# A fused attention and expert kernel: q's softmax subtraction, exponential and sum issued behind k's steps of the same unit

## The chip, the cores and the metric

The kernel runs on one core of one Trainium2 chip. The metric is the device time of one execution in microseconds, and the smaller is the better. Names of engines: PE is the matrix engine (TensorE), DVE is VectorE, ACT is ScalarE, POOL is GpSimd, SP is SyncE.

## What is computed

Three stages follow each other. Linear attention on q, k and v of 8 batches, 8 heads, 576 positions and 64 columns; a mixture of 8 experts with one expert per token; and a second, gated network. Cut to what matters:

```python
def _attn_ref(q, k, v):
    q_s = np.exp(q - np.max(q, axis=-1, keepdims=True))
    q_s = q_s / (np.sum(q_s, axis=-1, keepdims=True) + 1e-09)
    k_s = np.exp(k - np.max(k, axis=2, keepdims=True))
    k_s = k_s / (np.sum(k_s, axis=2, keepdims=True) + 1e-09)
    kv = np.einsum('bhsd,bhse->bhde', k_s, v)
    return np.einsum('bhsd,bhde->bhse', q_s, kv)
...
logits = x @ w_gate; e_idx = np.argmax(logits, axis=1)
out[mask] = gate_w * sigmoid(x @ w_output_gate)[e] * (np.maximum(x[mask] @ w1[e], 0) @ w2[e])
...
h = np.maximum(np.maximum(x @ w1, x @ w2), x @ w3); result = h @ w_out
```

The softmax of q goes over the 64 columns of a head, that of k over the 576 positions. x has 4608 tokens of 512 columns; an expert has 1024 hidden columns, the second network 768, and its weights come as float64 bits that the core decodes.

## The kernel before, in words

The attention works in units of half a batch's heads. Unit n is batch n // 2, half n % 2; even units are first halves, odd units second halves. The steps of a unit are small functions. For q: q_max, q_exp (L224 to 229: on DVE the subtraction of the maximum over 128 x 1280 elements, L228, then the exponential on ACT, L229), q_sum (L255 to 262, three DVE operations: the sum L259, and L260 and L261 on its 20 columns), q_norm (L264, DVE) and, for each of the two pairs of heads, q_tr (L315: PE transposes L320, ACT copy L327) and q_lo (L330, DVE L335: the low part of the transposed q). For k: k_max, k_tr (L231: PE transposes L236, DVE maximum L238 and two multiplications L241 that make dg), k_exp (L245: PE product of ones and dg L248, DVE subtraction L251, ACT exponential L253), kv_mm, kv_norm and kv_lo. Then x_mm (L337: PE products L353, ACT copies L361 and L363) and x_lo (L365, DVE L371) give the tokens of a pair, and logit_mm and logit_tr (PE L390, ahead of it ACT copies L384 and L385 in the last pair of a batch) feed the router, whose steps are route_1 to route_5; route_1 has six DVE instructions (L399 to L410), and route_5 is a POOL scatter into a table in memory (L489), five of them per batch.

Beside this the expert that most tokens of a batch chose is computed for all its tokens. Its work is cut in groups of 12 products of 128 x 288 (three per pair of operands, since each operand is split in a high and a low part). l1_group (PE L611) ends in an ACT operation (L616) and a DVE one (L617) that write h; l2_group (L629) reads h and ends on ACT (L634) in a batch's first half of groups and on DVE (L636) in its second half. 32 groups make a batch: 8 of l1, 8 of l2, and both again. The weights are split by ACT (L588) and POOL (L595). Between them dec_bits and dec_store decode weights of the second network (DVE L677 to 681 and L694, POOL L685, L686, L695).

One group is a slot. Behind each group moe_slot calls run_events, which issues all steps that a table has put at that slot. Engines work through their instructions in the order of issue; no scheduler moves them. The table is written by hand: START[n] = 16 n - 51 is a unit's slot 0, STEADY (L44) gives the offsets of its steps for units 4 to 15 and EARLY those of units 2 and 3; batch 0 has a list of its own. So k_tr stands at offset 0 of its unit, k_exp at 1, kv_mm and kv_norm at 6, q_norm at 8. The steps of a unit's second pair of heads come at offsets 15 to 19, which are offsets -1, 0, 1, 2 and 3 of the next unit: q_tr, q_lo, x_mm, x_lo and logit_mm of the previous unit. Behind the next even unit's offset 4 follow logit_tr and route_1. From offset 3 on, up to 10, the groups are l1 groups; those at -5 to 2 are l2 groups.

The table is read here:

```python
    FRONT = (q_max, q_exp, k_max, k_tr, k_exp, q_sum, kv_mm, kv_norm, kv_lo, q_norm)
    BACK = (q_tr, q_lo, x_mm, x_lo, logit_mm)
    for n, s0 in START.items():
        ...
        for d, f in zip(t[0], FRONT):
            if d is not None:
                at(s0 + d, f, b, hb)
```

Of the kernel before, what the change touches and what calls it, by code (L numbers as in the profile page):

```python
# [16 lines left out]
PSUM = bass.MemoryType.PSUM  # L17
# [11 lines left out]
CAP = 96  # L29
SLOT = 64  # L30
# [4 lines left out]

# batches whose attention output comes from plain float32 products instead of three with split operands
NFULL = 2

# The order of the work beside the experts' matrix products, in slots of one group of 12 products; a unit is
# half of a batch's heads. STEADY: slots after a unit's START for the steps in FRONT, and those in BACK for  # L40
# each pair of heads; EARLY: the same for the first units, from the first slot on. LOAD: a unit's loads.
# ROUTE: the router's steps after START of a batch's second unit, for batch 0 and 1 from the first slot on.
# DEC: pieces of the float64 weights, after START of even units, of odd units and of the last one.
STEADY = ((-4, -1, -4, 0, 1, 3, 6, 6, 7, 8), (10, 10, 13, 14, 15), (15, 16, 17, 18, 19))  # L44
EARLY = {
# [11 lines left out]
def tile_linear_attention__then__moe(  # L57
# [21 lines left out]

# [1 line left out]
    const = ctx.enter_context(tc.tile_pool(name="const", bufs=1))  # L81
# [24 lines left out]

# [1 line left out]
    es_moe = ExitStack()  # L108
# [20 lines left out]

# [1 line left out]
    def setup():  # L131
# [40 lines left out]

# [1 line left out]
    units = {}  # L174
# [197 lines left out]

    # the logits with tokens as columns: column tile c of the array takes tokens 128 c on; the last 64 follow on tile 0
    def logit_mm(b, hb, pr):
# [17 lines left out]

# [1 line left out]
    def route_1(b):  # L394
# [60 lines left out]
    def route_4(b):  # L455
        pool = nc.gpsimd
        r = rt[b]
        oh, cs, nm = r["oh"], r["cs"], r["nm"]
        cb = cbuf[b % 2]
        for c in range(4):  # L460
            pool.tensor_tensor(out=cb[:, c + 1], in0=cb[:, c], in1=cs[:, 0, c], op=ALU.add)
        n_b = n_all[:, E * b:E * b + E]
        s_b = st_all[:, E * b:E * b + E]
        pool.tensor_tensor(out=n_b, in0=r["cnt"], in1=nm[:, 0], op=ALU.mult)
        pool.tensor_copy(pad_a[:, 4:12], n_b)
        pool.tensor_tensor(out=pad_b[:, 4:12], in0=pad_a[:, 4:12], in1=pad_a[:, 3:11], op=ALU.add)
        pool.tensor_tensor(out=pad_a[:, 4:12], in0=pad_b[:, 4:12], in1=pad_b[:, 2:10], op=ALU.add)
        pool.tensor_tensor(out=pad_b[:, 4:12], in0=pad_a[:, 4:12], in1=pad_a[:, 0:8], op=ALU.add)
        pool.tensor_tensor(out=s_b, in0=pad_b[:, 4:12], in1=n_b, op=ALU.subtract)
        pool.tensor_tensor(out=s_b, in0=s_b, in1=base.to_broadcast([128, E]), op=ALU.add)  # L470
        pool.tensor_tensor(out=base, in0=base, in1=pad_b[:, 11:12], op=ALU.add)
        mo = sm.tile([128, 5, E], F32, tag="rmo", name="rmo")
        pool.tensor_tensor(out=mo, in0=oh, in1=nm.to_broadcast([128, 5, E]), op=ALU.mult)
        a = sm.tile([128, 5, E], F32, tag="ra", name="ra")
        pool.tensor_tensor(out=a, in0=cs[:, 1], in1=cb[:, 0:5], op=ALU.add)
        pool.tensor_tensor(
            out=a, in0=a, in1=s_b.rearrange("p (o e) -> p o e", o=1).to_broadcast([128, 5, E]), op=ALU.add
        )
        # the position of a token that leaves its batch's majority expert; BIG for the others
        pool.tensor_scalar(out=a, in0=a, scalar1=-float(BIG), scalar2=None, op0=ALU.add)  # L480
        pool.tensor_tensor(out=a, in0=a, in1=mo, op=ALU.mult)
        for w in (4, 2, 1):
            pool.tensor_tensor(out=a[:, :, 0:w], in0=a[:, :, 0:w], in1=a[:, :, w:2 * w], op=ALU.add)
        pi = sm.tile([128, 5], I32, tag="rpi", name="rpi")
        pool.tensor_scalar(out=pi, in0=a[:, :, 0], scalar1=float(BIG), scalar2=None, op0=ALU.add)
        r["pi"] = pi
# [6 lines left out]

# [1 line left out]
    events = {}  # L495
# [55 lines left out]

# [1 line left out]
    raw_t = {}  # L553
# [98 lines left out]

# [1 line left out]
    dec = deque((i, j) for j in range(8) for i in range(4))  # L654
# [12 lines left out]
    def dec_bits():  # L667
        if not dec_r:
            return
        i, j, raw = dec_r.popleft()  # L670
        lo, hi = raw[:, :, 0], raw[:, :, 1]
        f = dc_p.tile([128, 384], I32, tag="df", name="df")
        p = dc_p.tile([128, 384], I32, tag="dp", name="dp")
        a2 = dc_p.tile([128, 384], F32, tag="da", name="da")
        r = dc_p.tile([128, 384], F32, tag="dr", bufs=2, name="dr")
        # sign, exponent less 896 and the upper 20 bits of the mantissa
        vec.tensor_scalar(out=f, in0=hi, scalar1=0x07FFFFFF, scalar2=3,  # L677
                          op0=ALU.bitwise_and, op1=ALU.logical_shift_left)
        vec.scalar_tensor_tensor(out=f, in0=hi, scalar=-0x40000000, in1=f,
                                 op0=ALU.bitwise_and, op1=ALU.bitwise_or)  # L680
        vec.tensor_scalar(out=p, in0=f, scalar1=-0x00800000, scalar2=None, op0=ALU.bitwise_and)
        act(out=a2, in_=hi.bitcast(F32), func=ACTF.Abs)
        # the lower 32 bits, added with one rounding
        act(out=r, in_=lo.bitcast(U32), func=ACTF.Copy, scale=2.0 ** -52)
        nc.gpsimd.tensor_tensor(out=r, in0=r, in1=p.bitcast(F32), op=ALU.mult)  # L685
        nc.gpsimd.tensor_tensor(out=r, in0=r, in1=f.bitcast(F32), op=ALU.add)  # L686
        dec_m.append((i, j, a2, r))

    def dec_store():
        if not dec_m:  # L690
            return
        i, j, a2, r = dec_m.popleft()
        # under float32's range, by the upper word (0x38100000 and on, read as a float): zero
        vec.tensor_scalar(out=a2, in0=a2, scalar1=1.125 * 2.0 ** -15, scalar2=None, op0=ALU.is_ge)  # L694
# [9 lines left out]

# [1 line left out]
    m_all = [t.rearrange("p j n -> (p j n)").rearrange("(k f) -> k f", f=F2) for t in w32_d[0:3]]  # L706
# [29 lines left out]

    # ================= program =================
    with tc.manual_schedule():
# [95 lines left out]

# [1 line left out]
        sl = {}  # L836

        def fx_table():
# [43 lines left out]
            vec.tensor_reduce(out=sf[:, 0:4], in_=pr, axis=AX.X, op=ALU.add)  # L882
            # start = valid * (start0 + SLOT * j)
            vec.tensor_scalar(out=sf[:, 4:5], in0=jc, scalar1=float(SLOT), scalar2=None, op0=ALU.mult)
            vec.scalar_tensor_tensor(
                out=sf[:, 2:3], in0=sf[:, 4:5], scalar=sf[:, 3:4], in1=sf[:, 2:3], op0=ALU.mult, op1=ALU.add
            )
            # static start = min(start + CAP * (1 - valid), CAP)
            vec.tensor_scalar(
# [3 lines left out]
            vec.tensor_scalar(out=sf[:, 3:4], in0=sf[:, 4:5], scalar1=float(CAP), scalar2=None, op0=ALU.min)  # L893
            # trips of the general loop: 0 where the static slots cover everything
            nsl = incl[:, w - 1:w]
# [55 lines left out]

        # half a piece of a minority expert's weights: 256 rows of 512 columns
        def fx_w(e_reg, i):
# [33 lines left out]

        # the tokens' upper and lower parts side by side: the first pass multiplies both with the
        # weights' upper part, the second the upper part with the weights' lower part
        def fx_mm(ps, x, ws, kh):  # L990
# [9 lines left out]

        # adds the two parts and turns tokens to columns
        def fx_sum(raw):
# [62 lines left out]

        # steps between the groups of the second network; one that leaves its sum open in PSUM comes
        # only where the next step follows before that bank is needed again
        fix = deque((f, False) for f in (fx_table, fx_gather, fx_soft, lambda: None, fx_tr))
# [12 lines left out]

        # chunks: (sources of y, N, list of (scale, writer))
        def chunk_l2(c, hs, part=0):
# [20 lines left out]

        # chunk B holds the last 64 tokens of each batch, in two parts; the second carries the packed tokens
        order = [(c, 0) for c in range(B)] + [(B, 0), (B, 1)]
# [113 lines left out]
```

## Time and profile before

| what | value |
|---|---|
| time, median of 3 runs | 1252.41 us (1251.85 to 1254.42) |
| span of the profiled execution | 1248.6 us |
| between the two | 3.8 us |
| PE busy | 1193.2 us, 96% |
| DVE busy | 647.8 us, 52% |
| ACT busy | 447.0 us, 36% |
| POOL busy | 380.4 us, 30% |

The span is that of one execution, recorded by the hardware profiler; the durations below come from it. The profile has one time per run of instructions, the wait ahead of it and what ended that wait. A busy time counts an instruction from its start to its end, also when something held it in between. A granted clock of 1.00 is PE's full speed, 2.4 GHz, and 0.50 is 1.2 GHz.

### The profile page before, as it was taken

What the parts mean: (1) busy time and instruction counts of PE and PEld (TensorE: products, weight loads), DVE (VectorE), ACT (ScalarE), POOL (GpSimd) and SP (SyncE); (2) the same over time, 40 slices, a digit from 0 to 9 for tenths busy, and PEclk for the clock granted to TensorE, in tenths of its full rate; (3) what the DMA queues carried; (4) which work ended last, traced back from release to release, by engine and by line L of the source; (5) the groups of instructions that cost most, each with busy time, mean ns of one, the idle gap of its engine ahead of it and who ended that gap; (6) DMA issues with size and microseconds to landing.
All of it is one profiled execution on the core that took longest, in us unless ns stands there. A gap on an engine that the chain in (4) does not pass through costs nothing. (4 is left out here: it accounts for less than half of the span.)

```text
span 1248.6 us, 19283 instructions
## 1 busy us (share of the span) xinstructions
PE 1193.2 (96%) x7518; PEld 1054.4 (84%) x7518; DVE 647.8 (52%) x1161; ACT 447.0 (36%) x864; POOL 380.4 (30%) x466
## 2 busy tenths in 40 slices
PE   4699999999999999999999999999999999999996
PEld 3598998989899898999888888888888888888995
DVE  7779787787878789534442414132331313232211
ACT  2463554546454554534331223122232213221211
POOL 1257767676776667772002000000000000000000
PEclk9799999999999999999999999999999999999998
DMA  6776555675665544353512121211222111210001
GB/s 167 183 198 175 166 176 159 175 214 148 202 202 164 170 128 148 123 188 99 169 35 79 36 67 52 83 44 34 85 68 76 46 56 51 51 51 1 35 17 24
DMA packets 141455, 135.68 MB, mean 109 GB/s; under 512 B 70045, under 2 KB 104637, under 8 KB 140336
## 3 DMA queue, kind: packets, MB, share of 16 engines
q1 hardware_dynamic: 139648, 134.01, 36.1%
q8 instruction: 61, 1.00, 0.3%
q0 software_dynamic: 1712, 0.39, 0.2%
q14 instruction: 34, 0.28, 0.1%
HBM read 106.99 MB, written 27.62 MB: 108 GB/s over the span
## 5 line engine op out<-in xcount | busy, mean ns | idle before, releaser
L813 PE MATMUL pm<-yh,wf 128*128 128x512 f32 (+2 forms) x2160 | 464.8, 375 | 0.0
L813 PEld LDWEIGHTS pm<-yh,wf 128*128 128x128 f32 x2160 | 385.9, 188 | 72.5
L629 PE MATMUL yp<-h,w 128*128 128x288 f32 x1536 | 226.3, 303 | 0.2 <-DVE h L617 0.2
L611 PE MATMUL hp<-xs,w 128*128 128x288 f32 x1536 | 218.9, 299 | 0.0
L629 PEld LDWEIGHTS yp<-h,w 128*128 128x128 f32 x1536 | 212.1, 192 | 3.6 <-DVE h L617 0.5
L611 PEld LDWEIGHTS hp<-xs,w 128*128 128x128 f32 x1536 | 208.1, 190 | 2.8 <-POOL w L595 0.2
L595 POOL TENSOR_TENSOR w<-stg,w 128x512 fp32r<-128x512 f32 x126 | 179.4, 1427 | 77.0 <-ACT w L588 74.9
L820 DVE TENSOR_TENSOR tm<-tm,pm 128x512 f32<-128x512 f32 (+2 forms) x60 | 38.6, 643 | 256.6 <-ACT tm L819 152.3
L1077 POOL DMA_INDIRECT out_dram<-oc,ftb x1 | 1.0, 983 | 548.4 <-ACTq L1149 548.4
L831 PE MATMUL op<-wo,hc 128*128 128x512 f32 (+1 forms) x666 | 152.8, 390 | 0.0
L831 PEld LDWEIGHTS op<-wo,hc 128*128 128x128 f32 (+1 forms) x666 | 124.5, 187 | 26.3
L819 ACT ACTIVATE tm<-pm 128x512 f32<-128x512 f32 (+2 forms) x60 | 33.7, 562 | 230.9 <-PE pm L813 230.2
L617 DVE SCALAR_TENSOR_TENSOR h<-hp,h 128x288 fp32r<-128x288 f32 x128 | 56.6, 451 | 58.8 <-ACT h L616 58.5
L616 ACT ACTIVATE h<-hp 128x288 fp32r<-128x288 f32 x128 | 52.2, 408 | 84.6 <-PE hp L611 84.2
L588 ACT ACTIVATE w<-stg 128x512 fp32r<-128x512 f32 x128 | 78.8, 621 | 0.0
L823 ACT ACTIVATE hc<-tm 128x512 fp32r<-128x512 f32 (+2 forms) x60 | 35.8, 597 | 93.9 <-DVE tm L821 93.9
L824 DVE TENSOR_TENSOR hc<-tm,hc 128x512 fp32r<-128x512 f32 (+2 forms) x60 | 38.9, 649 | 39.8 <-ACT hc L823 39.8
L833 ACT ACTIVATE oc<-op,tsrc 128x512 f32<-128x512 f32 x32 | 22.1, 689 | 101.9 <-PE op L831 101.9
L489 POOL DMA_INDIRECT tab_d<-tsrc,rpi x40 | 45.9, 1147 | 37.5 <-DMA tab_d<-tsrc,rpi 26.2
L685 POOL TENSOR_TENSOR dr<-dr,dp 128x384 f32<-128x384 f32 x32 | 32.5, 1015 | 53.2 <-ACT h L616 37.3
L228 DVE TENSOR_TENSOR q<-q,qm 128x1280 f32<-128x1280 f32 x15 | 42.7, 2849 | 0.0
L821 DVE TENSOR_TENSOR tm<-tm,pm 128x512 f32<-128x512 f32 (+2 forms) x60 | 38.6, 644 | 7.0 <-DVE tm L820 0.9
(219 smaller groups left out, 1179.1 us busy)
## 6 DMA issues: line engine op xcount, KB each, us to landing
stg<-in_moe_w_dram SPq DMA_DIRECT2D x31, 1024.0 KB, 5.7
fw<-in_moe_w_dram SPq DMA_DIRECT2D x24, 512.0 KB, 3.8
v<-in_v_dram SPq DMA_DIRECT2D x80, 128.0 KB, 4.8
draw<-in_moe_w_dram SPq DMA_DIRECT2D x24, 384.0 KB, 4.1
y_d<-y SPq DMA_DIRECT2D x32, 288.0 KB, 2.7
k<-in_k_dram SPq DMA_DIRECT2D x16, 512.0 KB, 5.2
q<-in_q_dram SPq DMA_DIRECT2D x16, 512.0 KB, 6.6
yr<-y_d SPq DMA_DIRECT2D x8, 1024.0 KB, 5.2
```

The source lines that it names most:

```text
L228: eng.tensor_tensor(out=qt, in0=qt, in1=u["qm"].to_broadcast([128, 20, D]), op=ALU.subtract)
L489: nc.gpsimd.indirect_dma_start(out=tab_d[:, :], out_offset=bass.IndirectOffsetOnAxis(ap=rt[b]["pi"][:, c:c + 1], axis=0), in_=tsrc[:, b, c ...
L588: act(out=t[:, 0], in_=src, func=ACTF.Copy)
L595: eng.tensor_tensor(out=t[:, 1], in0=src, in1=t[:, 0].bitcast(F32), op=ALU.subtract)
L611: mm(ps, w[:, a, kk], xp[b, kk][:, c, cs], start=(n == 0), stop=(n == 11))
L616: act(out=h[:, 0, cs], in_=ps, func=ACTF.Relu)
L617: vec.scalar_tensor_tensor(out=h[:, 1, cs], in0=ps, scalar=0.0, in1=h[:, 0, cs].bitcast(F32), op0=ALU.max, op1=ALU.subtract,)
L629: mm(ps, w[:, a, f], ht[f][:, c, cs], start=(n == 0), stop=(n == 11))
L813: mm(pp[m][:, 0:n], wf[f][:, a, m, kk], ys[kk][:, c, 0:n], start=(kk == 0 and i == 0), stop=(kk == 3 and i == 2))
L820: vec.tensor_tensor(out=tv, in0=tv, in1=pp[1][:, 0:n], op=ALU.max)
L824: vec.tensor_tensor(out=h[:, 1, 0:n], in0=tv, in1=h[:, 0, 0:n].bitcast(F32), op=ALU.subtract)
L831: mm(ps[0:m], hs[f][:, a, 128 * t:128 * t + m], wo[f][:, c], start=(i == 0), stop=(i == 17))
```

## The change

In STEADY the offset of q_exp goes from -1 to 2 and that of q_sum from 3 to 5. All else stays (the other lines of the diff take comments out, and the line numbers hold for both).

```diff
-STEADY = ((-4, -1, -4, 0, 1, 3, 6, 6, 7, 8), (10, 10, 13, 14, 15), (15, 16, 17, 18, 19))
+STEADY = ((-4, 2, -4, 0, 1, 5, 6, 6, 7, 8), (10, 10, 13, 14, 15), (15, 16, 17, 18, 19))
```

The order of issue changes on DVE and ACT in units 4 to 15; on PE, POOL and SP it is the same. First, DVE around offset 0 of an odd unit, before. The rows name line, operation, tiles and shape; q and qm are the unit's q and its maximum, qTs the transposed q of the previous unit's second pair, dg k's maxima on a diagonal, xs the tokens, y and h the expert's tiles.

```order
L371 TENSOR_TENSOR xs<-xr,xs 128x576
L636 TENSOR_TENSOR y<-yp,y 128x288
L228 TENSOR_TENSOR q<-q,qm 128x1280
L636 TENSOR_TENSOR y<-yp,y 128x288
L335 TENSOR_TENSOR qTs<-qT,qTs 128x576
L238 TENSOR_REDUCE m_3381<-kT 128x2
L241 TENSOR_SCALAR dg<-ident,m_3381 128x128 x2
L636 TENSOR_TENSOR y<-yp,y 128x288
L251 TENSOR_TENSOR k<-k,kB 128x1280
L636 TENSOR_TENSOR y<-yp,y 128x288
L371 TENSOR_TENSOR xs<-xr,xs 128x576
L617 SCALAR_TENSOR_TENSOR h<-hp,h 128x288
```

The same place after the change, from the q_lo of the previous unit on:

```order
L335 TENSOR_TENSOR qTs<-qT,qTs 128x576
L238 TENSOR_REDUCE m_3379<-kT 128x2
L241 TENSOR_SCALAR dg<-ident,m_3379 128x128 x2
L636 TENSOR_TENSOR y<-yp,y 128x288
L251 TENSOR_TENSOR k<-k,kB 128x1280
L636 TENSOR_TENSOR y<-yp,y 128x288
L371 TENSOR_TENSOR xs<-xr,xs 128x576
L228 TENSOR_TENSOR q<-q,qm 128x1280
L617 SCALAR_TENSOR_TENSOR h<-hp,h 128x288
L677 TENSOR_SCALAR df<-draw 128x384
L679 SCALAR_TENSOR_TENSOR df<-draw,df 128x384
L681 TENSOR_SCALAR dp<-df 128x384
```

q's subtraction stood between two additions of y and ahead of q_lo and dg; now it stands behind q_lo, dg, k's subtraction and x_lo, and right ahead of the first h.

Second, DVE at offsets 2 to 5 of an even unit, after the change, from k's subtraction to q's sum:

```order
L251 TENSOR_TENSOR k<-k,kB 128x1280
L371 TENSOR_TENSOR xs<-xr,xs 128x576
L228 TENSOR_TENSOR q<-q,qm 128x1280
L617 SCALAR_TENSOR_TENSOR h<-hp,h 128x288 x2
L399 TENSOR_REDUCE rm<-lg 128x5
L401 TENSOR_TENSOR rd<-lg,rm 128x40
...
L617 SCALAR_TENSOR_TENSOR h<-hp,h 128x288
L259 TENSOR_REDUCE qs<-q 128x20
L260 TENSOR_SCALAR qs<-qs 128x20
L261 RECIPROCAL qs<-qs 128x20
L677 TENSOR_SCALAR df<-draw 128x384
```

Before, L259 to L261 stood between the first and the second L617 there; now they stand behind route_1's six instructions and the third.

Third, ACT at the same place, as one piece of the difference:

```order
 L588 ACTIVATE w<-stg 128x512
 L634 ACTIVATE y<-yp 128x288
+L229 ACTIVATE q<-q 128x1280
 L616 ACTIVATE h<-hp 128x288
 L384 ACTIVATE lgt<-lgT 128x128
```

q's exponential now stands ahead of the first h of the l1 groups and of the copies of the logits, which the logit transpose on PE reads; it stood three l2 groups earlier.

## Rows read from the trace of the kernel before

**Rows 1.** What PE waited for: us in total, times, longest us
```profile
PE xT L353 <- DVE qTs L335: 14.2, 6, 2.7
PE kB L248 <- DVE dg L241: 13.1, 9, 8.0
```
**Rows 2.** Line 228 (ns min/median/max); timeline of unit 9: start us, us, what, [idle <-releaser]
```profile
L228 DVE TENSOR_TENSOR q<-q,qm x15: 1481/2302/4318, 17.7 to 473.3; 128x1280 f32<-128x1280 f32 x15
...
260.64 1.40 POOL L489 DMA_INDIRECT tab_d<-tsrc,rpi  x1 [0.16 <-issue]
261.38 4.30 DVE L228 TENSOR_TENSOR q<-q,qm 128x1280 f32<-128x1280 f32 x1
262.07 1.30 POOL L595 TENSOR_TENSOR w<-stg,w 128x512 fp32r<-128x512 f32 x1
263.32 1.02 POOL L695 TENSOR_TENSOR dr<-da,dr 128x384 f32<-128x384 f32 x1
...
266.78 1.81 PE L353 MATMUL xT<-qTs,kvs 128*128 128x288 f32 x6 [2.33 <-DVE qTs L335]
```
**Rows 3.** Window of unit 9: from:to, us, busy per engine, granted PE clock, DMA share, GB/s
```profile
266.70:268.40 1.70, 1.62 (x7) 1.57 (x7) 1.67 (x5) 0.81 (x2) 1.19 (x1) 0.50 0.87 254
```
**Rows 4.** PE timeline: k's transposes and first l1 group, units 5, 8, 9, 15
```profile
120.89 0.38 PE L236 MATMUL kT<-ident,kmx 128*128 128x128 f32 x2
130.54 0.70 PE L611 MATMUL hp<-xs,w 128*128 128x288 f32 x4
...
229.13 0.38 PE L236 MATMUL kT<-ident,kmx 128*128 128x128 f32 x2
233.75 0.43 PE L611 MATMUL hp<-xs,w 128*128 128x288 f32 x2
...
262.49 0.38 PE L236 MATMUL kT<-ident,kmx 128*128 128x128 f32 x2
271.20 1.08 PE L611 MATMUL hp<-xs,w 128*128 128x288 f32 x7
...
474.43 0.38 PE L236 MATMUL kT<-ident,kmx 128*128 128x128 f32 x2
482.36 0.82 PE L611 MATMUL hp<-xs,w 128*128 128x288 f32 x5
```
**Rows 5.** Timeline of unit 8 to the logit transpose
```profile
229.88 1.28 ACT L229 ACTIVATE q<-q 128x1280 f32<-128x1280 f32 x1 [1.70 <-DVE q L228]
...
233.75 0.75 DVE L371 TENSOR_TENSOR xs<-xr,xs 128x576 fp32r<-128x576 f32 x1
...
235.74 2.64 POOL L595 TENSOR_TENSOR w<-stg,w 128x512 fp32r<-128x512 f32 x2 [2.69 <-ACT w L588]
...
235.86 0.40 ACT L616 ACTIVATE h<-hp 128x288 fp32r<-128x288 f32 x1
...
236.30 0.20 ACT L385 ACTIVATE lgt<-lgT 32x64 f32<-32x64 f32 x1
...
237.56 0.33 PE L390 MATMUL lg<-ident,lgt 128*128 128x64 f32 x2
```
**Rows 6.** Timeline of unit 8, from the first h to q_tr
```profile
236.29 0.46 DVE L617 SCALAR_TENSOR_TENSOR h<-hp,h 128x288 fp32r<-128x288 f32 x1 [1.79 <-ACT h L616]
...
247.34 0.46 DVE L617 SCALAR_TENSOR_TENSOR h<-hp,h 128x288 fp32r<-128x288 f32 x1 [0.42 <-ACT h L616]
...
247.71 1.72 DVE L268 TENSOR_TENSOR qn<-q,qs 128x1280 f32<-128x1280 f32 x1
...
249.88 0.60 PE L320 MATMUL qT<-ident,qn 128*128 128x128 f32 x4
```
**Rows 7.** Timeline of unit 9, from offset 2 to q_tr
```profile
270.18 0.99 POOL L489 DMA_INDIRECT tab_d<-tsrc,rpi  x1 [2.30 <-DMA tab_d<-tsrc,rpi]
...
284.35 1.48 DVE L268 TENSOR_TENSOR qn<-q,qs 128x1280 f32<-128x1280 f32 x1
...
286.52 0.60 PE L320 MATMUL qT<-ident,qn 128*128 128x128 f32 x4
```

## The prediction

> **What bounds the kernel now.** I read the share of each engine first (in the table above): PE is busy 96% of a span of 1248.6 us and no other engine over 52%. So the time is PE's work plus its waits plus what it loses at a lower clock, and the view to open next is the list of what PE waited for. In the stretch that the change touches it has two lines [rows 1]: x_mm (L353) waits six times for q_lo (L335), 14.2 us in all, and k_exp's product of ones (L248) waits nine times for dg (L241); one of the nine, at the very start, is 8.0 long, so the other eight hold (13.1 - 8.0) / 8 = 0.64 each. Everything else in the interleaved part is hidden by PE. The question is only where these waits come from and what takes their place.
>
> The timeline of unit 9 shows the first line's cause [rows 2]. VectorE's subtraction q_exp (L228) starts at 261.38 while POOL's scatter (L489) is under way, and takes 4.30. Its fastest sister takes 1.48, the median 2.30 (the group of line 228). Behind it in the row of VectorE stands the previous unit's q_lo, and the x products wait 2.33 for it. Such a wait comes once in each odd steady unit (5, 7, 9, 11, 13, 15): six. The windows add that PE runs at a granted clock of 0.50, the 1.2 GHz level, in the slot after it [rows 3].
>
> What one such place costs is read on PE, from k's transposes (L236, slot 0) to the first l1 group after them (L611, slot 3), the same work in each unit [rows 4]. Even unit 8: 233.75 - 229.13 = 4.62. Unit 9: 8.71, so 4.09 lost; the first odd one, unit 5: 9.65, 5.03 lost; the last, unit 15: 7.93, 3.31 lost. With the mean of first and last, 4.2, six units lose 25.2 us. It holds the waits of 14.2, and 11.0 (1.8 a unit) of lower clock and of short waits for dg behind them.
>
> **What the change removes.** In the twelve steady units the subtraction stands three slots later, behind the previous unit's q_lo, k's maximum, dg, k's subtraction and x_lo. q_lo then has nothing of q ahead of it, so the whole 25.2 goes if the new place does not rebuild it: **-25.2**. No instruction is added or dropped on any engine, and no DMA, SP or POOL instruction is moved. The twelve exponentials (L229) and three-step sums (L259 to L261) are the same work in another place.
>
> **What it adds, even units.** At the new place the row of unit 8 reads [rows 5]: x_lo (L371) starts at 233.75 and takes 0.75, so it ends at 234.50. The subtraction may then start; POOL's L595 starts only at 235.74, so I take the undisturbed 1.48: 235.98. The exponential takes 1.28: 237.26. On ScalarE the first h (L616) and the two copies of the logits stand behind it; now they run from 235.86 to 236.50, which is 0.64, so they end at 237.90. PE's logit transpose (L390) starts at 237.56: a new wait of **0.4** (0 if the exponential is passed a little earlier, 0.64 if wholly uncovered).
>
> On VectorE the first h's second half (L617) waited already 1.79 for ScalarE, until 236.29 [rows 6]. Now its ScalarE half ends at 237.26 + 0.40 = 237.7: 1.4 late. Until now the sums of q filled the waits for the next two h; now they come behind the third, and I count 0.6 and 0.2 more of idle there. So q_norm (L268) comes 2.2 late, less the 0.42 of idle in the row ahead of it: 1.8. It ended at 247.71 + 1.72 = 249.43; it would end at 251.2, 251.9 if another 0.7 of the sum is uncovered. Its reader, q_tr (L320), starts at 249.88, with the 0.4 above at 250.28: a wait between 0.95 and 1.6; I take **1.2**.
>
> **Odd units.** The same subtraction and exponential arrive, but the router's six steps (L399 to L410), which even units have at slot 4, do not. q_norm's slack in unit 9 is 286.52 - (284.35 + 1.48) = 0.69 [rows 7], against 0.45 in unit 8. VectorE gains 1.48 of subtraction and about 1.4 of waiting for exponential and h, and about 1.4 of idle closes: 1.48 less 0.69 is **0.8** of wait at q_tr (0 if more idle closes; 2.2 if none does).
>
> **Both.** Once per pair of units the dg multiplications, no longer behind q's subtraction, meet POOL's split, as in the eight short waits of 0.64 [rows 1]: **0.5** (0 to 0.64). And the l2 groups eight slots on read every h; with VectorE late the last one may not be there: none now, at worst the subtraction's 1.48; I take **0.6**, under the middle, because VectorE's idle shrinks the delay by then.
>
> **Sum.** Per pair 0.4 + 1.2 + 0.8 + 0.5 + 0.6 = 3.5; six pairs 21.0; -25.2 + 21.0 = **-4.2**. The profiled execution's span of 1248.6 becomes 1244.4; around the span lie 3.8 to the median of the three runs, 1252.4, so the time becomes **1248.2**. That is 0.34%; about 0.2%, 2.5 us, is what a measurement of this kernel can tell from nothing.
>
> **A row and a rule.** The row: L228 started at 261.38, before L595 started at 262.07 and L695 at 263.32, and yet both of them ran at 1.30 and 1.02 and the subtraction ended only after them [rows 2]. So a VectorE operation that comes while POOL's scatter is under way can be passed by what POOL does next. The Trainium skill (SBUF — State Buffer, section "SBUF: two separate sides") says that the port pair which VectorE and GpSimd share is an exclusive lock, held for a whole instruction by whichever starts first. By that rule the subtraction would have been kept only for the rest of the scatter, and at its new place for at most the one split that is under way; the row says that it can be three instructions, which makes the collision dearer. The sum takes no collision at the new place; the dear one is rival D.
>
> **Rivals.**
> *A, slower: the clock falls at the new waits.* Place: q_tr in the even units. In unit 9 the clock fell behind a wait of 2.33 [rows 2, 3]; if 1.2 is enough, each even unit pays between 1.3 (1.8 of the odd place less a dg wait of 0.5) and 1.8; with 1.6, six pay 9.6: -4.2 + 9.6 = +5.4, **1257.8**. For: one single stop was enough there. Against: the one here is half as long, and no row shows the clock behind such a one. It decides at a length between the two, 1.2 and 2.33.
> *B, no change: the waits only move.* If the sums of q are as uncovered as the upper ends above (1.6, 0.8 and more of 1.48), the new waits come to 4.2 a pair, and 25.2 stands against 25.2: **1252.4**. For: VectorE's work between slot 2 and q_norm grows by all that is taken from the stretch ahead. Against: its 1.79 idle [rows 6] is room.
> *C, the whole gain.* Idle time absorbs all but the 0.4 at the logits: -25.2 + 2.4 = -22.8, **1229.6**. Against: q_norm's slack is 0.45 and 0.69 only.
> *D, the collision moves along.* In odd units, scatter and two POOL operations are passed again at slot 2: 4.30 - 1.48 = 2.8, six times 16.9: +12.7, **1265.1**. For: the scatters of the batch before still run there, one at 270.18 in unit 9 [rows 7]. Against: as in unit 8 the subtraction is asked 0.75 after the first l1 group starts, with the loss gone at 271.20 - 4.09 + 0.75 = 267.9, and POOL stands idle for a DMA in the 2.30 before 270.18, from 267.9 on. It decides whether the subtraction comes before that scatter or during it, a matter of 2.3 us. By the page's rule it would be held by one POOL operation at most, 1.30 [rows 2], in six units 7.8: +3.6.
>
> **Chances.** Forecast 0.48 (its own range 1243 to 1251: half of the open terms up or down), A 0.17, B 0.22, C 0.05, D 0.08. Faster by over 0.2%: 0.44 of the forecast and C, 0.49. Within: B and the upper end of the forecast, 0.04, together 0.26. Slower: A and D, 0.25. The range runs from 1238.0, where half of the new waits is absorbed, to 1259.0, just over A; left out are C, D and the tails of B and the forecast.
>
> **What would show it.** Right: L228 near 1.5 in the twelve units; no wait of x_mm for q_lo; 4.6 from k's transposes to the first l1 group in odd units; new lines in PE's waits, q_tr for q_norm (about twelve, 0.8 to 1.2) and the logit transpose for ScalarE (0.4), with a granted clock of 1.00 behind them. Wrong: waits of 2 us for q_norm or 0.50 of clock behind them (A); new waits of 25 us (B); hardly any (C); L228 over 3 (D).

## The result, and the profile after

The changed kernel is slower: 1263.88 us median (1260.88 to 1266.29, 4 runs) against 1252.13 beside it (1250.94 to 1254.42, 4 runs), a ratio of 1.0093 with a 95% interval of 1.0074 to 1.0113. The profiled execution has a span of 1261.4 us, 12.8 more than before. The first lines of its page:

```profile
span 1261.4 us, 19284 instructions
PE 1197.4 (95%) x7518; PEld 1056.3 (84%) x7518; DVE 647.9 (51%) x1161; ACT 443.3 (35%) x864; POOL 371.7 (29%) x466
```

PE is busy for 4.2 us more (it ran slower in places, as the windows below show) and the rest of the 12.8 is waiting. What PE waited for, in us, times and longest us:

```profile
PE qT L320 <- DVE qn L268: 27.7, 13, 3.1
PE kB L248 <- DVE dg L241: 10.2, 3, 8.0
```

The line of x_mm for q_lo [rows 1] is gone; a line twice its length stands in its place, q_tr waiting for q_norm, which before was there once (2.7 us, in the early units). q's subtraction is 1.48 in all units now (before, [rows 2]), and unit 9 goes from k's transposes to the first l1 group in 272.84 - 268.15 = 4.69 us, where an even unit took 4.62 before [rows 4]. So what the change was to remove is gone. The group of line 228 (columns as in [rows 2]), then PE's timeline in unit 9 (start us, us, what, idle before):

```profile
L228 DVE TENSOR_TENSOR q<-q,qm x15: 1478/1484/1486, 17.8 to 494.7; 128x1280 f32<-128x1280 f32 x15
```
```profile
268.15 0.38 PE L236 MATMUL kT<-ident,kmx 128*128 128x128 f32 x2
...
272.84 0.42 PE L611 MATMUL hp<-xs,w 128*128 128x288 f32 x2
...
291.30 1.11 PE L320 MATMUL qT<-ident,qn 128*128 128x128 f32 x4 [2.99 <-DVE qn L268]
```

Then unit 9 loses 2.99 at q_tr. Where q_norm's lateness comes from is seen in the timelines of DVE and POOL, offsets 3 to 8 of unit 9, put together by time:

```profile
277.39 1.32 POOL L595 TENSOR_TENSOR w<-stg,w 128x512 fp32r<-128x512 f32 x1
277.58 1.36 DVE L677 TENSOR_SCALAR df<-draw 128x384 int32<-128x384 int32 x1
278.88 0.99 POOL L489 DMA_INDIRECT tab_d<-tsrc,rpi  x1 [0.17 <-issue]
279.57 1.84 DVE L681 TENSOR_SCALAR dp<-df 128x384 int32<-128x384 int32 x1
279.88 1.30 POOL L595 TENSOR_TENSOR w<-stg,w 128x512 fp32r<-128x512 f32 x1
...
283.47 1.01 POOL L686 TENSOR_TENSOR dr<-dr,df 128x384 f32<-128x384 f32 x1
283.57 0.94 DVE L260 TENSOR_SCALAR qs<-qs 128x20 f32<-128x20 f32 x1
284.43 1.29 POOL L595 TENSOR_TENSOR w<-stg,w 128x512 fp32r<-128x512 f32 x1
284.74 1.20 DVE L694 TENSOR_SCALAR da<-da 128x384 f32<-128x384 f32 x1
...
289.17 2.08 DVE L268 TENSOR_TENSOR qn<-q,qs 128x1280 f32<-128x1280 f32 x1
```

Four short operations take 5.34 us here; the shortest times of the same lines are 0.30, 0.36, 0.18 and 0.34, so 4.2 of it is time in which they were held while POOL ran, and q_norm has 0.6 more. (Not all of this is new: L694 took 0.72 here before.) The group of line 681, before and then after, shows the newest part (ns min/median/max): it was hardly held before.

```profile
L681 DVE TENSOR_SCALAR dp<-df x32: 359/360/487, 100.3 to 532.6; 128x384 int32<-128x384 int32 x32
```
```profile
L681 DVE TENSOR_SCALAR dp<-df x32: 359/361/1840, 101.8 to 545.4; 128x384 int32<-128x384 int32 x32
```

Unit 8 is the even case: q_norm is late too, but only by 1.31 at its reader (timelines of DVE and PE).

```profile
253.19 2.22 DVE L268 TENSOR_TENSOR qn<-q,qs 128x1280 f32<-128x1280 f32 x1
...
255.47 0.66 PE L320 MATMUL qT<-ident,qn 128*128 128x128 f32 x4 [1.31 <-DVE qn L268]
```

The windows right behind the two waits (columns as in [rows 3]): in unit 8 the granted clock stays at 1.00, in unit 9 it is 0.50 and then 0.67.

```profile
256.20:257.95 1.75, 1.75 (x13) 1.69 (x13) 1.26 (x7) 1.09 (x4) 1.45 (x7) 1.00 1.05 365
292.70:295.65 2.95, 2.95 (x13) 2.95 (x13) 2.05 (x4) 0.65 (x1) 2.87 (x3) 0.50 0.83 221
295.70:297.95 2.25, 2.25 (x13) 2.25 (x13) 1.66 (x3) 1.80 (x4) 1.34 (x2) 0.67 0.97 292
```

A sum by units closes the account. From the group of offset 0 to that of the next unit, the six even units (4 to 14) take 202.5 us before and 212.7 after, the six odd ones (5 to 15; the last up to its offset 16) 222.3 and 224.9: 10.2 and 2.6, together the 12.8 of the span. The same two sums are given for each run below. They come from one profiled execution of each kernel, so a difference of a few us between two of them can be chance.

### The profile page after: what moved, and what is told of

The parts are those of the page before. It is cut to its first block, busy times and chain, and to the rows that moved or that the text cites. A ratio compares the mean times of both kernels' runs of the same rounds, so it can differ in the third digit from the quotient of the medians.

```text
span 1261.4 us, 19284 instructions
## 1 busy us (share of the span) xinstructions
PE 1197.4 (95%) x7518; PEld 1056.3 (84%) x7518; DVE 647.9 (51%) x1161; ACT 443.3 (35%) x864; POOL 371.7 (29%) x466
## 5 line engine op out<-in xcount | busy, mean ns | idle before, releaser
L629 PE MATMUL yp<-h,w 128*128 128x288 f32 x1536 | 229.3, 306 | 0.3 <-DVE h L617 0.3
L629 PEld LDWEIGHTS yp<-h,w 128*128 128x128 f32 x1536 | 215.4, 195 | 3.4 <-DVE h L617 0.5
L595 POOL TENSOR_TENSOR w<-stg,w 128x512 fp32r<-128x512 f32 x126 | 174.4, 1387 | 95.8 <-ACT w L588 94.4
L820 DVE TENSOR_TENSOR tm<-tm,pm 128x512 f32<-128x512 f32 (+2 forms) x60 | 38.7, 644 | 257.5 <-ACT tm L819 148.2
L831 PEld LDWEIGHTS op<-wo,hc 128*128 128x128 f32 (+1 forms) x666 | 124.5, 187 | 26.4
L617 DVE SCALAR_TENSOR_TENSOR h<-hp,h 128x288 fp32r<-128x288 f32 x128 | 56.8, 453 | 58.3 <-ACT h L616 57.0
L489 POOL DMA_INDIRECT tab_d<-tsrc,rpi x40 | 43.3, 1083 | 39.5 <-DMA tab_d<-tsrc,rpi 27.1
L320 PE MATMUL qT<-ident,qn 128*128 128x128 f32 x128 | 23.4, 310 | 28.4 <-DVE qn L268 27.7
L320 PEld LDWEIGHTS qT<-ident,qn 128*128 128x128 f32 x128 | 15.2, 154 | 33.5 <-DVE qn L268 30.7
```

What stands on the lines that cost most here:

```text
L320: nc.tensor.transpose(ps[:, 128 * c:128 * c + 128], qv[:, c], ident)
L489: nc.gpsimd.indirect_dma_start(out=tab_d[:, :], out_offset=bass.IndirectOffsetOnAxis(ap=rt[b]["pi"][:, c:c + 1], axis=0), in_=tsrc[:, b, c ...
L595: eng.tensor_tensor(out=t[:, 1], in0=src, in1=t[:, 0].bitcast(F32), op=ALU.subtract)
L617: vec.scalar_tensor_tensor(out=h[:, 1, cs], in0=ps, scalar=0.0, in1=h[:, 0, cs].bitcast(F32), op0=ALU.max, op1=ALU.subtract,)
L629: mm(ps, w[:, a, f], ht[f][:, c, cs], start=(n == 0), stop=(n == 11))
L820: vec.tensor_tensor(out=tv, in0=tv, in1=pp[1][:, 0:n], op=ALU.max)
```

## The experiments

The first theory after the result: even units lose 1.7 each by themselves, and odd units lose all that they gained because POOL holds the short operations that now stand between x_lo and q_norm. Each experiment's own two theories, numbered 1 and 2, are in the expectation that stands with it. Unless another edit is shown, a kernel differs from the changed one in the table, and where odd units have one of their own, by this:

```diff
-            t = STEADY
+            t = STEADY_ODD if n % 2 else STEADY
```

Kernels measured together share their runs of the kernel before, whose median was 1250.5 to 1251.3 there; a ratio is to those.

| run | time, us | ratio (95%) | even units, us | odd units, us |
|---|---|---|---|---|
| before | 1252.1 | 1 | 202.5 | 222.3 |
| the change | 1263.9 | 1.0093 (1.0074 to 1.0113) | 212.7 | 224.9 |
| odd units alone | 1251.0 | 1.0000 (0.9974 to 1.0025) | 201.9 | 223.2 |
| even units alone | 1263.5 | 1.0079 (1.0055 to 1.0104) | 212.7 | 225.3 |
| pieces late | 1283.3 | 1.0238 (1.0205 to 1.0270) | 261.6 | 197.5 |
| scatters late | 1262.6 | 1.0084 (1.0062 to 1.0106) | 231.4 | 203.9 |
| odd, pieces and loads late | 1263.9 | 1.0100 (1.0072 to 1.0129) | 218.4 | 217.4 |
| change, pieces and loads late | 1263.3 | 1.0089 (1.0065 to 1.0114) | 223.4 | 212.9 |
| before, pieces and loads late | 1282.5 | 1.0253 (1.0220 to 1.0286) | 231.1 | 223.7 |
| before, scatters late | 1267.4 | 1.0125 (1.0099 to 1.0152) | 227.3 | 212.5 |
| change, scatters wide | 1251.2 | 1.0003 (0.9988 to 1.0018) | 213.7 | 211.9 |
| odd, scatters wide | 1240.4 | 0.9922 (0.9896 to 0.9947) | 203.3 | 211.1 |
| before, scatters wide | 1258.8 | 1.0063 (1.0039 to 1.0087) | 203.1 | 230.4 |
| change, sum at 3 | 1246.3 | 0.9959 (0.9944 to 0.9975) | 208.3 | 210.8 |
| odd, scatters chosen | 1252.8 | 1.0017 (1.0008 to 1.0026) | 205.0 | 220.5 |
| sum at 5 alone | 1262.6 | 1.0096 (1.0065 to 1.0127) | 212.3 | 224.8 |
| odd, sum at 3 | 1244.4 | 0.9949 (0.9933 to 0.9965) | 205.8 | 212.7 |
| odd, sum at 3, scatters wide | 1241.0 | 0.9924 (0.9898 to 0.9950) | 205.7 | 210.2 |

### The two kinds of unit apart

Edit: the row of the kernel before for the even units, and for the odd ones in the second run.

```diff
+STEADY = ((-4, -1, -4, 0, 1, 3, 6, 6, 7, 8), ...
+STEADY_ODD = ((-4, 2, -4, 0, 1, 5, 6, 6, 7, 8), ...
```

> Only the odd steady units (5 to 15) have q's subtraction and exponential at offset 2 and the sum at 5; even units stand as before the change. Theory 1 (what the change costs in odd units is made there, on VectorE, between x_lo and q_norm, by short operations that POOL holds up): the six odd units behave as in the changed kernel, wait about 3.0 us each for q_norm with a low clock behind, and lose what they gained: before + 2 to 3 us, 1254 to 1256. Theory 2 (the odd loss needs the even units' lateness, which is handed on from unit to unit): odd units wait under 1 us and the time falls to about 1252 - 26 + 5 = 1231.

> Only the even steady units (4 to 14) are changed; odd units stand as before the change. Theory 1 (each even unit pays 1.3 at q_tr and 0.4 at the logit transpose, independent of the odd ones): 6 x 1.7 to 1.9, before + 10, about 1262; the odd units keep their waits of x_mm for q_lo (14 us) and no wait of 3 us for q_norm appears. Theory 2 (lateness is handed on): the odd units change too, the sum differs from 10 by more than 3.

PE's waits, odd units alone and then even units alone (in these kernels and the next two, line numbers are one higher):

```profile
PE qT L321 <- DVE qn L269: 16.1, 6, 3.1
```
```profile
PE xT L354 <- DVE qTs L336: 15.7, 6, 2.6
...
PE qT L321 <- DVE qn L269: 10.6, 7, 2.7
```

Each kind keeps its loss without the other: even units lose 10.2 in both runs that change them, odd ones end about where they were. Lateness is not handed on. Theory 1 was right in size for the even units; for the odd ones alone it gave 2 to 3 us more than came, which the interval can't tell from nothing.

### The decoding pieces, and the scatters, out of the way

```diff
-DEC = ((5, 10), (3, 8, 11), (18, 26))
+DEC = ((5, 10), (8, 11, 14), (18, 26))
```

> The changed kernel with the decoding pieces of odd units at offsets 8, 11, 14 in place of 3, 8, 11, so that none stands between q's subtraction and q_norm. Theory 1 (the short decoding operations, held up beside POOL, are over half of the odd units' lateness: 1.2 of work and 2.6 of holding): q_norm comes 3.8 earlier, the 3.0 wait at q_tr and the clock's fall in odd units go, even units keep 1.3: 1263.9 - 29 = about 1235. Theory 2 (subtraction, exponential and late h alone make odd units late): the wait stays over 1.5 and the time over 1250. A third case: the pieces collide at their new place and PE waits elsewhere.

The odd units came out as theory 1 says: 197.5, units 5 to 13 at 32.65 each, no wait for q_norm. But the piece at 14 waited on VectorE for its DMA, and q_lo behind it, so that PE waited for q_lo six times, 29.8 us. That the DMA had queued behind the unit's loads is a reading, which the next runs try. It is the third case; more was lost than won. The timeline of DVE, the piece ahead of offset 0 of unit 8:

```profile
239.78 0.36 DVE L678 TENSOR_SCALAR df<-draw 128x384 int32<-128x384 int32 x1 [6.15 <-DMA draw<-in_moe_w_dram]
```

The other hand at it leaves VectorE's row alone and moves POOL's scatters:

```diff
-            at(r2 + 5 + 2 * c, route_5, b, c)
+            at(r2 + 5 + 2 * c + (14 if 1 < b < 7 else 0), route_5, b, c)
```

> The changed kernel with the router's five scatters of batches 2 to 6 issued 14 slots later, at offsets 9 to 17 of the odd unit in place of -5 to 3; all work on VectorE stays where it is. Theory 1 (holding by POOL): with no scatter beside them the piece's third step (L681) falls from 1.84 to 0.36 and the whole holding from 3.7 to about 2 us or less; the wait for q_norm in units 7 to 15 falls from 3.0 to 1.5 or less, the clock may stay up: 1263.9 - 5 x (1.5 to 3) = 1249 to 1256. Theory 2 (it is VectorE's own work): waits stay at 3.0 and the time at 1264.

Odd units 7 to 15 fall to 33 to 34 us and wait 0.03 or less for q_norm, though VectorE has the same work in the same order: in the odd units theory 2 is out. In unit 9 the piece's first and third step take 0.35 and 0.36 (1.36 and 1.84 above); L260 is still held, 1.25. The timelines of DVE and PE there:

```profile
278.07 0.36 DVE L682 TENSOR_SCALAR dp<-df 128x384 int32<-128x384 int32 x1
...
285.70 2.11 DVE L269 TENSOR_TENSOR qn<-q,qs 128x1280 f32<-128x1280 f32 x1
...
287.86 0.66 PE L321 MATMUL qT<-ident,qn 128*128 128x128 f32 x4
```

The same scatters cost the even units, where they now meet the router's steps and dg, 18.7 us, so that the time is 1262.6 and not the 1249 to 1256 expected.

### Pieces late with the loads later too

```diff
-            at(LOAD.get(n, START.get(n - 2, 0) + 9), load_unit, b, hb)
+            at(LOAD.get(n, START.get(n - 2, 0) + 13), load_unit, b, hb)
```

> Odd units as in the changed kernel, even units as before it, the odd units' decoding pieces at offsets 8, 11, 14, and each unit's loads issued at offset 13 of the unit two before in place of 9, so that the load of the piece at 14 doesn't queue behind them (it did in the run with the pieces late: 8 us of wait for its DMA). Theory 1 (holding of the short operations made the odd loss): odd units take 32.7 to 33 us, even ones 33.4, no wait over 1 us for q_norm or q_lo: before - 6 x 4 = about 1226. Theory 2 (late loads were not the cause of the 20 us lost there, the piece at 14 itself collides ahead of the next q_lo): x_mm waits 1 to 3 us for q_lo in even units, 1235 to 1250.

> The changed kernel in all units, pieces at 8, 11, 14 and loads at 13 as in the run beside it. Theory 1: as that run plus the even units' 1.7 to 1.9 each: about 1226 + 10 = 1236, odd units 33, even 35.3. Theory 2: 1245 to 1260.

> Control: the kernel before with the same move of pieces and loads and q's steps where they were. If the place of the pieces matters only together with q's move, the waits of x_mm for q_lo stay (14 us, six times, the subtraction 4.3) and the time is that of before within 3 us. If pieces or loads are worth something by themselves, it is 1235 to 1247.

All three missed. In the odd units another operation took the pieces' place beside POOL: q_norm in units 5, 7 and 13, and in unit 9 kv_lo (L313, 4.57 in place of 0.41). The timeline of POOL and DVE in units 7 and 9 of the first of these runs:

```profile
211.15 0.99 POOL L489 DMA_INDIRECT tab_d<-tsrc,rpi  x1 [0.92 <-DMA tab_d<-tsrc,rpi]
212.16 3.76 POOL L595 TENSOR_TENSOR w<-stg,w 128x512 fp32r<-128x512 f32 x3
212.33 4.96 DVE L268 TENSOR_TENSOR qn<-q,qs 128x1280 f32<-128x1280 f32 x1
...
283.55 0.99 POOL L489 DMA_INDIRECT tab_d<-tsrc,rpi  x1 [1.07 <-DMA tab_d<-tsrc,rpi]
284.04 4.57 DVE L313 TENSOR_TENSOR kvs<-kvraw,kvs 128x256 fp32r<-128x256 f32 x1
284.56 3.77 POOL L595 TENSOR_TENSOR w<-stg,w 128x512 fp32r<-128x512 f32 x3
```

Both were held for three splits that ran behind a scatter without a gap. In the control the even units take 28.6 more: x_mm waits 1.7 to 2.5 for q_lo and k_exp 1.6 for dg in units 6 to 14. In unit 6 the piece stands right ahead of q's subtraction and q_lo, with 1.06 of wait for its DMA (6.15 in the row above, with the loads early) and 2.3 of work; whether the piece or the later loads make the price was not parted. The two holds led to a sharper theory: a scatter waits on POOL for the DMA of the one before, splits pile up behind it, and VectorE is held for the whole run.

### The scatters alone

> The kernel before with the scatters of batches 2 to 6 issued 14 slots later. If a scatter under way lets POOL's next operations pass the subtraction, L228 in units 7 to 15 falls from 4.3 to 1.5 to 2.8, unit 5 keeps it, and the waits of x_mm for q_lo there go (-20 us); the even units pay about 18 for the scatters' new place, as they did with the changed kernel, so the time is about 1249. If the splits alone hold it, L228 stays over 3.5 in odd units.

L228 in the odd units 7 to 15 fell from 4.3 to 2.2, as expected, but the time is 1267.4 and not about 1249. The odd units gained 9.8 in place of 20, because k_exp's wait for dg grew to 1.4 there, and the even ones paid 24.8 in place of 18.

```diff
-            at(r2 + 5 + 2 * c, route_5, b, c)
+            at(r2 + 5 + (4 if 1 < b < 7 else 2) * c, route_5, b, c)
```

> The changed kernel with the five scatters of batches 2 to 6 four slots apart in place of two (offsets -5, -1, 3, 7, 11 of the odd unit). Theory 1 (each scatter waits on POOL for the DMA of the one before, splits and scatters pile up behind it and run without a gap, and VectorE is held for the run): with the waits gone the runs are one or two long, the holding between x_lo and q_norm falls from 4 to under 2 us in units 7 to 15, and the 3.0 wait for q_norm to under 1.5: 1264 - 5 x 3 = about 1250. Theory 2 (single operations of POOL hold as much): holding stays over 3, the time over 1258.

> Only the odd units changed, with the wide scatters. Theory 1: odd units at 33 to 34.5 in place of 37 to 38.5, even units 33.4 as before: about 1251 - 5 x 3 = 1236. Theory 2: as the run with the odd units alone, 1251.

> The kernel before with the wide scatters. Theory 1: q's subtraction (L228) in units 7 to 15 falls from 4.3 to 1.5 to 2.8 and the wait of x_mm for q_lo from 2.4 to under 1: about 1251 - 5 x 3 = 1236. Theory 2: L228 stays at 4.3, because a scatter still stands at offset -1 with its two followers: 1251.

With the change theory 1 gave the time to 1 us: 1251.2, odd units 7 to 15 at 34.9. That close a hit is in part luck: their wait for q_norm fell to 0.87, but q_norm is now held longer (3.13) and a wait for dg of 1.06 is new. With the odd units alone it gave 1236 and 1240.4 came, 0.8% faster than before: the first version that beats both kernels. In the kernel before both theories failed (1236 and 1251 expected, 1258.8 measured). The scatter at offset -1 stayed, with a longer run behind it (timeline of POOL and DVE, unit 9):

```profile
264.69 1.40 POOL L489 DMA_INDIRECT tab_d<-tsrc,rpi  x1 [0.16 <-issue]
265.43 5.52 DVE L228 TENSOR_TENSOR q<-q,qm 128x1280 f32<-128x1280 f32 x1
266.11 1.30 POOL L595 TENSOR_TENSOR w<-stg,w 128x512 fp32r<-128x512 f32 x1
267.36 1.02 POOL L695 TENSOR_TENSOR dr<-da,dr 128x384 f32<-128x384 f32 x1
268.33 1.26 POOL L595 TENSOR_TENSOR w<-stg,w 128x512 fp32r<-128x512 f32 x1
```

So the distance of the scatters does not decide by itself; the run that a held operation meets does.

### The hold by itself

Two kernels of small trials, no part of the computation. One trial of the second kernel, cut short; the first kernel has one copy on ACT ahead and no scatter:

```python
act(out=src, in_=fl[:, 0:4], func=ACTF.Copy)
act(out=fl[:, 0:256], in_=fl[:, 256:512], func=ACTF.Copy)
scatter()
for i in range(k):
    pool.tensor_tensor(out=w[i], in0=w[4], in1=fl, op=ALU.add)
vec.tensor_reduce(out=flat[:, 0:4], in_=fl[...], axis=AX.X, op=ALU.max)
op()                           # the operation in question
```

> Not the computation: 90 small trials, output zero. In each, ACT releases VectorE and POOL at once; POOL runs 0 to 4 tensor_tensor operations of 128 x 512 back to back (about 1.3 us each), VectorE a reduction of 0.3 us and then one operation: a subtraction of 128 x 1280 as q's, a tensor_scalar of 20 columns as q_sum's, one of 384 int32 columns as the decoding's, a tensor_reduce of 128 x 1280, and an operation on PSUM as h's. In a sixth trial of each, POOL's two operations are parted by an ACT copy. Theory 1 (POOL's whole uninterrupted run goes first): the subtraction takes 1.5 + 0.9, then 1.3 more for each further POOL operation (2.4, 3.7, 5.0, 6.3), and 2.4 with the gap; the two tensor_scalars 1.1 to 5.0 in the same steps; the reduction and the PSUM operation stay the same. Theory 2 (the port is given by instruction): the same 2.4 for 1 to 4 operations, with POOL's second operation late by 1.5.

> Not the computation: 80 small trials, output zero, as in the first of this kind, but POOL starts with a scatter (1.0 us) and goes on with 0 to 3 tensor_tensor operations without a gap; VectorE asks just before the scatter ends. Theory 1, as it now stands (a scatter under way or just ended lets the whole of POOL's run go first, up to its first gap): the subtraction takes about 1.5, 2.7, 4.0, 5.3 for 0, 1, 2, 3 operations behind the scatter, the two tensor_scalars 0.2 to 4 in the same steps, 2.7 with a gap behind the first, and without a scatter 2.3 whatever the length; asked in the middle of the run (the late trials) it still waits for the end with the scatter, and for one operation without. Theory 2 (by instruction, scatter or not; the long holds in the kernel have another cause): 2.3 to 2.7 for 1 to 3 operations, and POOL's next operation is late instead. Reduction and PSUM operation unchanged in both.

Without a scatter, four POOL operations in a row, the subtraction (L45) asked in the first (timeline of POOL and DVE):

```profile
27.55 6.17 POOL L74 TENSOR_TENSOR w<-w,fl 128x512 f32<-128x512 f32 x4 [1.13 <-ACT fl L68]
27.89 2.26 DVE L45 TENSOR_TENSOR bo<-big,m 128x1280 f32<-128x1280 f32 x1
```

The same view of the second kernel, a scatter ahead of three:

```profile
22.72 0.99 POOL L77 DMA_INDIRECT tab<-src,pi  x1 [2.11 <-ACT src L83]
23.18 5.61 DVE L45 TENSOR_TENSOR bo<-big,m 128x1280 f32<-128x1280 f32 x1
23.74 3.69 POOL L92 TENSOR_TENSOR w<-w,fl 128x512 f32<-128x512 f32 x3
```

In the first, the subtraction takes 2.2 to 2.3 for one to four operations, and it is POOL's second that is late (four take 6.17 where 5.0 is their own): theory 2, and the length of the run alone is out. In the second, it takes 3.18, 4.41 and 5.61 for one, two and three operations behind the scatter, 3.20 when a gap follows the first, and the three take 3.69, not delayed at all: theory 1 as it then stood. The same kernel has its controls: 1.49 with nothing behind the scatter, 2.46 with three operations and no scatter. Asked 1.5 us after the scatter has ended, in the second of three operations, the subtraction still waits for the end of the run (3.63; 1.70 without a scatter). The tensor_scalars go the same way (1.86, 3.10, 4.31 and 2.03, 3.27, 4.48); the reduction stays at 1.49 and the operation on PSUM at 0.46.

### The sum of q

```diff
+STEADY = ((-4, 2, -4, 0, 1, 3, 6, 6, 7, 8), ...
+STEADY_ODD = ((-4, 2, -4, 0, 1, 3, 6, 6, 7, 8), ...
```

> The changed kernel with q's sum back at offset 3: the move of subtraction and exponential alone. Theory 1 (even units pay for 1.5 of subtraction and 0.7 of holding that now stand between x_lo and q_norm; odd ones for operations that meet a run of POOL behind a scatter, whichever they are): even units stay at 35.2 us, odd ones at 37 to 38.5, time 1260 to 1266. Theory 2 (the later sum is what makes q_norm late): even units fall to 33.5 to 34.5, odd ones lose 1 to 2 us less, time 1240 to 1252.

1246.3, which is theory 2. The move of subtraction and exponential alone is a gain of 0.41%; the sum's later place turns it into a loss. The odd units take 210.8 in place of 224.9: they wait 1.1 to 1.9 for q_norm in place of 3.0. In unit 9 L677 takes 0.30 and L681 0.55 (1.36 and 1.84 with the whole change), while L260 is held a little longer (1.29). The opposite half:

```diff
+STEADY = ((-4, -1, -4, 0, 1, 5, 6, 6, 7, 8), ...
+STEADY_ODD = ((-4, -1, -4, 0, 1, 5, 6, 6, 7, 8), ...
```

> The kernel before with only q's sum moved from offset 3 to 5, subtraction and exponential left at -1. Theory 1 (the later sum costs by itself: at 3 it fills the wait for the second h, at 5 it is work ahead of q_norm, and in odd units it meets POOL there): even units come 0.9 to 1.1 later at q_norm against 0.45 of slack, 0.5 each; odd units 1 to 2 later against 0.69, about 1: before + 3 to 10, 1254 to 1261, with short waits of q_tr for q_norm. Theory 2 (the later sum costs only together with the subtraction at its new place, since there is idle time without it): no wait for q_norm, 1251.

1262.6: the even units lose as much (212.3) as with the whole change. The timeline of DVE in unit 8 of this run:

```profile
241.27 0.46 DVE L617 SCALAR_TENSOR_TENSOR h<-hp,h 128x288 fp32r<-128x288 f32 x1 [1.79 <-ACT h L616]
243.19 0.46 DVE L617 SCALAR_TENSOR_TENSOR h<-hp,h 128x288 fp32r<-128x288 f32 x1 [1.46 <-ACT h L616]
...
245.22 0.46 DVE L617 SCALAR_TENSOR_TENSOR h<-hp,h 128x288 fp32r<-128x288 f32 x1 [0.40 <-ACT h L616]
245.59 1.48 DVE L259 TENSOR_REDUCE qs<-q 128x20 f32<-128x1280 f32 x1
...
254.06 2.22 DVE L268 TENSOR_TENSOR qn<-q,qs 128x1280 f32<-128x1280 f32 x1
```

Before, the sum ran in the 1.46 that VectorE here waits for the second h, and q_norm took 1.72 [rows 6]; now it stands ahead of q_norm as work, and q_norm comes where POOL holds it 0.5 longer. The causes don't add up in the even units: the sum alone costs them 9.8, subtraction and exponential alone 5.8, both together 10.2. The odd units, whose waits for q_lo stay, take 2.5 more with the sum alone and have no wait for q_norm.

### Towards the best version

> Only the odd units changed, and the scatters of batches 1 to 6 at offsets -5, -2, 3, 9, 13 of the odd unit, so that none stands ahead of dg (offset 0), of the decoding piece (3 to 5) or of q_norm (8). Theory 1: in the run with wide scatters units 7 to 15 still paid 0.9 to 1.0 at dg and 1.1 at q_norm, both held behind a scatter, and unit 5 all of it; with these gone 1240.4 - 5 x 2 - 3 = about 1228; if only one of the two goes, 1233. Theory 2 (the holds come with the splits, not with scatters): 1240 again.

1252.8, a miss. The offsets were chosen in the same line:

```diff
+            at(r2 + 5 + ((0, 3, 8, 14, 18)[c] if 0 < b < 7 else 2 * c), route_5, b, c)
```

dg and the decoding piece were free, but x_lo, q's subtraction, the sum's second step and q_norm itself were each held by splits (1.2, 1.1, 1.1 and 0.6 in unit 9), and q_tr waited 2.0 to 2.3 in units 7 to 15. With scatters moved, POOL's splits stand elsewhere too; a place can't be chosen for the scatters alone.

```diff
+STEADY = ((-4, -1, -4, 0, 1, 3, 6, 6, 7, 8), ...
+STEADY_ODD = ((-4, 2, -4, 0, 1, 3, 6, 6, 7, 8), ...
```

> Only the odd units have subtraction and exponential at offset 2, with the sum at 3; even units as before. Theory 1 (units don't hand their lateness on): odd units 34.5 to 35.2 as in the run with the sum at 3 in all units, even ones 33.4: 1246.3 - 6 x 1.0 = 1240. Theory 2: the even units' change moves when POOL meets the odd units' operations, and the time lies over 1246.

> As the run beside it, with the scatters four slots apart. Theory 1 (sum and scatters act on the same lateness at q_norm, 0.9 to 1.1 in the run with wide scatters, and 0.9 is what the earlier sum takes off): odd units 33.7 to 34, 1240.4 - 5 x 0.9 = about 1236. Theory 2 (the operations that now come earlier meet other runs of POOL): 1240 or more.

1244.4 and 1241.0: better than both kernels, but 4 to 5 over what adding up the parts gave. In the first the even units 10 and 12 waited 1.5 and 0.7 at dg, which is theory 2 in small; in the second the wait for q_norm is gone in the odd units 7 to 15, and an l2 group waits 1.0 for a late h instead. The odd units with the scatters four slots apart, with the sum at 3 or at 5, are the fastest found, 1240 to 1241.

## Why the prediction was wrong

It said 1248.2 and a gain of 4.2; a loss of 11.8 came, outside the range, though the forecast's mechanism was mostly there.

**What is removed (25.2): right.** The wait for q_lo is gone in all units, with what it cost behind it. An odd unit without any such wait takes 32.65 in the run with the pieces late; six of them before were 222.3, so 26.4 stood there. One reading was too simple: the clock did not fall in all six. In unit 15 of the kernel before, x_mm waited 2.31 too, and the window behind it is at 1.00 (columns as in [rows 3]):

```profile
478.70:481.70 3.00, 2.51 (x16) 2.25 (x17) 2.48 (x5) 2.08 (x4) 1.12 (x1) 1.00 0.63 215
```

**Even units (0.4 at the logits, 1.2 at q_tr): right in size.** The slot of the logit transpose grew from 2.06 to 2.42, the wait at q_tr is 1.31: 10.2 in six units against 9.6. The share of each cause was not: the text let the subtraction bring most of the lateness and the sum's move 0.8 of idle. The two halves show the sum alone enough for the whole 1.3; with the sum at 3 and the subtraction at 2, 0.1 is left of it. So that 1.2 came so near is luck.

**Odd units (0.8 at q_tr): the step that failed.** "VectorE gains 1.48 of subtraction and about 1.4 of waiting for exponential and h, and about 1.4 of idle closes" counted each operation at its own time, and the prediction's sum took no collision at the new place: holding of the operations between x_lo and q_norm stood in it at nothing, though an operation held for 2.8 stood in [rows 2]. In unit 9, q_norm ends 17.08 after x_lo (274.17 to 291.25) in place of 12.70 (273.13 to 285.83). Of these 4.4 us, 1.5 is the subtraction; holding is up by 1.1 (L677), 1.5 (L681), 0.8 (L260), 0.5 (L694) and 0.6 (L268), together 4.4; idle is down by 1.2, and 0.3 lies in the other operations. So the wait is 2.99, and behind it come slots at a granted clock of 0.50 and 0.67: 25.2 + 2.6 = 27.8 us in six units where 4.8 stood. The run with the scatters late, in which VectorE's work is the same and the wait is gone, shows the holding to be the cause, and the one with the pieces late, at 32.65 a unit, agrees. With the sum at 3, half of the 27.8 goes (14.1), so half of it came with the sum's later place.

**dg (0.5) and late h (0.6): did not come.** PE's line for dg shrank from nine waits to three, all of them before unit 4, and the groups wait 0.3 for h once. The eight short waits of 0.64 had been misread as one kind: two of them, 1.1 each, come in the first 16 us, and those of the steady units are 0.3 to 0.5. The terms now close: odd units 23.0 over the forecast, even ones 0.6 over, dg and h 6.6 under, together the 17.0 between -4.2 and the span's +12.8.

**Rivals.** D had the mechanism (POOL's run passes a VectorE operation in odd units), by luck about the time that came (1265.1) and the wrong victim: the subtraction itself came free at its new place, as the argument against D said, and the operations behind it were caught. Its chance was put at 0.08 because only the moved operation was asked about. A is half shown: the clock did fall, but behind 3.0 in the odd units 5 to 13, and 1.3 in the even units did not do it. The length of a wait does not decide it alone, as unit 15 above shows. B's sign, new waits of 25 us, came to the letter (27.7 less the early 2.7), but neither its break-even (the span grew by 12.8) nor its cause: POOL lengthened the waits, not uncovered sums. C did not happen. The listed signs could not tell these apart: waits over 2, a clock of 0.50 and 25 us of new waits stood for A and B, and D's sign, L228 over 3, stayed away though its mechanism came.

## What to carry to other kernels

When a long operation is moved, price what its old place sheltered and what its new place pushes: here none of the twelve moved subtractions was held, and the short operations behind them met another engine's run. Before moving an operation off an idle stretch, see what it filled there; the sum at 3 was free because VectorE had to wait for h anyway. And run the parts of a change apart: one half of this one was a gain of 0.4%, the other a loss of 1%.

## What the runs showed of the hardware

In the trials a VectorE subtraction of two operands in SBUF and two forms of tensor_scalar were held by POOL's tensor_tensor. Without a scatter, one POOL operation under way holds the subtraction and the next one of POOL waits in turn: 2.20 to 2.27 for one operation to four, 1.49 for none. The Trainium skill (SBUF — State Buffer, section "SBUF: two separate sides") describes this as an exclusive lock for a whole instruction; these trials agree. Behind a scatter they don't: the operation waits for every POOL operation that follows without a gap, 1.2 to 1.3 us each, and POOL is not delayed (3.18, 4.41, 5.61; 1.49 when nothing follows the scatter). In the kernel such runs held one operation for up to 5.5 in place of 1.48. A reduction, and an operation with one operand in PSUM, were not held in either. Why a scatter has this effect, no run here tells.
